# Attention, top-1 and Sinkhorn mixtures of experts in one kernel: the shared block's steps, the branch for further blocks and two weight loads in other places

## The chip, the cores and the metric

One NeuronCore of a Trainium2 chip runs the whole kernel. The metric is the device time of one execution in microseconds (us), the median of several runs; lower is better. TensorE is PE in the profile (its weight loads PEld), VectorE is DVE, ScalarE is ACT, GpSimd is POOL, SyncE is SP. SP and POOL also issue the transfers (DMAs): SP the plain ones, POOL the gathers and scatters by index.

## The reference

Attention with rotary positions over 2 batches, 8 heads, 576 positions of 64 values; its output, 1152 tokens of 512 values, goes through two layers of 8 experts. This change lies in and around the first of them:

```python
logits = xn @ en.T / tau                     # cosine of token and expert
expert_idx = np.argmax(logits, axis=1)
gate_w = probs[np.arange(N), expert_idx]
for e in range(E):
    mask = expert_idx == e
    h = np.maximum(x[mask] @ w1[e], 0.0)     # 512 -> 1024
    out[mask] = gate_w[mask, None] * (h @ w2[e])   # 1024 -> 512
```

The second layer (the dense one) puts every token through all 8 experts with weights from 8 Sinkhorn rounds.

## The kernel before, in words

**Stages.** Attention and routing come first (up to about 183 us of the span), then the expert blocks of the first layer (`run_blocks`, to about 340 us), then the dense layer (`dense_experts`, the rest). The instructions of PE, DVE, ACT and POOL stand in the order in which the Python code records them (`tc.manual_schedule`); each engine runs its own list in that order and waits where an operand isn't there.

**Blocks.** The tokens of an expert are cut into blocks of 128. Ten blocks (i = 0 to 9) always run; a branch (`tc.If`, L971) runs further ones if there are more than ten. Here there are not: after block 9 every engine jumps over that code. Experts with few tokens share one more block, 32 rows for each of four experts: the **shared block** (names with `quad`).

**One pass of the loop for block i** does on PE: L1(i), the first product (`block_l1`, L756, 24 matmuls); xt(i+1), four transposes of the next block's tokens (`block_x`, L743); L2(i-1), the second product of the block before (`block_l2`, L786); ht(i), eight transposes of L1's result (`block_turn`, L771). The products are made of fp32 values split in two: ACT copies the high parts (`whi` L728 of the weights, `xh` L746, `hh` L773) and DVE subtracts the low parts (`wlo` L721, `xl` L747, `hl` L774). Per pass there are two `whi`/`wlo` pairs for the next block's first weights and two for block i's second weights. DVE's two `hl` come behind the last two `wlo` of a pass.

**PSUM.** xt, ht and all small products of this stage take turns in two banks (tag "x"). A bank is free again when ACT and DVE have read it.

**The shared block.** `quad_fetch(s)` (s = 0 to 7) has SP load four 512 KB pieces of weights (`qw`) into a ring of eight tiles, so part s+2 can't be loaded before part s is multiplied. `place_quad` computes on DVE which token goes to which row (`slot`, L555), lets PE make the indices (ten small matmuls with `qv`, L561), and DVE writes them to `idx`. `block_in(NB)` has POOL gather the tokens, `quad_tokens` transposes them (`qxt`, L824), `quad_product(s)` is part s of the products (q0 to q7, L837, eight matmuls), `quad_relu` and `quad_turn` (L844, L851) come between parts 3 and 4. Before the change the places are computed in pass 1, and part s stands behind L2 in pass s+2; part 7 stands behind L1(9). Part s+1's load (`quad_fetch(i)` in pass i) is issued a whole pass and more ahead of its use.

**SP's queue** in a pass: the first weights of block i+2, the second weights of block i+1 (each 4 x 512 KB, left out when the expert stays the same; but SP still waits, at the first and third of them, until DVE's `wlo` has read the buffer), then the shared block's load. From pass 6 on `next(dense)` mixes in the dense layer's first steps: `fetch1(0)` and `fetch1(1)` load first weights (`raw1` from `w1b`, 512 KB a step), `prep_plain` splits them (L1032, L1033), and `fetch1(2)`, `fetch1(3)` load the next two as soon as their buffers are read.

**The change of stage.** Behind the branch SP loads four quarters of the layer's result (`g` from `yd`, L1151) once the last scatter into `yd` (POOL, L793) has landed; PE runs 28 matmuls to no purpose but activity (L1160) and then transposes the first quarter (L1163).

Of the kernel before, what the change touches and what calls it, by code (L numbers as in the profile page):

```python
# [10 lines left out]
F32 = mybir.dt.float32  # L11
# [38 lines left out]
def fused_kernel(ctx, tc, qk, vv, tab, cst, emb, tau, w1a, w2a, wg, w1b, w2b, out):  # L50
# [11 lines left out]
    def bank(tag, bufs, name, shape=(128, 512)):  # L62
        return ps[0].tile(list(shape), F32, tag=tag, bufs=bufs, name=name)
# [319 lines left out]
    def tmp(name, shape, dt=F32):  # L383
        return rt.tile(shape, dt, name=name)
# [5 lines left out]
    def over(v, axis, shape):  # L390
        return v.unsqueeze(axis).to_broadcast(shape)
# [151 lines left out]
            G.tensor_copy(qv[:, :, x], col(name))  # L543
        G.memset(qv[:, :, 5], 1.0)

    def place_quad(bank_):

        z, qi = tmp("z", [QT, E]), tmp("qi", [BLK, 2])
        V.tensor_scalar(z, grp, float(GS), 1024.0, op0=ALU.mult, op1=ALU.add)
        V.scalar_tensor_tensor(z, inq, -1024.0, z, op0=ALU.mult, op1=ALU.add)  # L550
        V.tensor_tensor(ws, ohb[:, :, :NQ], z.unsqueeze(1).unsqueeze(1).to_broadcast([QT, B, NQ, E]), op=ALU.mult)
        V.tensor_reduce(blk, ws, axis=AX.X, op=ALU.add)
        V.tensor_tensor(blk, blk, rk, op=ALU.add)
        sl = [QT, B * NQ, BLK]
        V.tensor_tensor(slot.rearrange("p b t n -> p (b t) n"), over(col("iota"), 1, sl),  # L555
                        over(blk.rearrange("p b t -> p (b t)"), 2, sl), op=ALU.is_equal)
        p = bank_()
        for b in range(B):
            for c in range(NQ):
                m, n = TW[c], b * NQ + c  # L560
                T.matmul(p[:, :6], slot[:m, b, c], qv[:m, n], start=(n == 0), stop=(n == B * NQ - 1))  # L561
        V.tensor_reduce(qi[:, 0:1], p[:, 0:2], axis=AX.X, op=ALU.add)
        V.tensor_copy(idx[:, 0, NB:], qi[:, 0:1])
        V.tensor_reduce(gate[:, NB:], p[:, 2:5], axis=AX.X, op=ALU.add)
        V.tensor_scalar(qi[:, 1:2], p[:, 5:6], 1.0, cs[:, COLS["slot"]], op0=ALU.subtract, op1=ALU.mult)
        V.tensor_tensor(qi[:, 1:2], qi[:, 0:1], qi[:, 1:2], op=ALU.subtract)
        V.tensor_copy(idx[:, 1, NB:], qi[:, 1:2])
# [253 lines left out]
    def quad_tokens():  # L821
        pt = bank("x", 2, "qxt")
        for k in range(KD_):
            T.transpose(pt[:, k * 128:(k + 1) * 128], quad["xb"][:, k * 128:(k + 1) * 128], ident)  # L824
        quad["x"] = mp.tile([128, F], F32, tag="qx", bufs=1, name="qx")
        A.activation(quad["x"][:, :DM], pt, AF.Copy)
# [19 lines left out]
    def quad_turn():  # L846
# [5 lines left out]
            A.activation(t[:, n * 512:(n + 1) * 512], pt, AF.Copy)  # L852
        quad["x"] = t

    def run_blocks(lo, hi, xb=None, w1=None, w2=None):

        def expert(i, raws, src, n):
# [9 lines left out]
        with tc.manual_schedule(engines=ORDERED):  # L867
# [10 lines left out]
            for i in range(lo, hi + 1):  # L878
                begin, here, more = i == 0, i < hi, i + 1 < hi

                if here:
                    p = block_l1(x, w1)
                if lo == 0 and i == 2:
                    quad_tokens()
                elif lo == 0 and i == 6:
                    quad_turn()
                elif lo == 0 and i == 9:
                    quad_product(7)
                    block_out(NB, quad["p", 0])
                if begin:  # L890
                    next(gated)
# [13 lines left out]
                if begin:  # L905
                    h = block_turn(hn)
                    split_low(raw2p[1], *w2[1])
                    w2 = pieces(w2)
                    expert(1, raw2, w2a, 256)
                    next(gated)  # L910
                    quad_fetch(0)
                    quad_constants()
                if i + 2 < hi and len(xb) < i + 3 - lo:
                    xb.append(block_in(i + 2))
                if begin:
# [7 lines left out]
                    y = block_l2(h, w2, (lambda: turned.append(block_turn(hn))) if i == hi - 1 else None, i == hi)  # L923
                if i == 1:
                    place_rest(lambda: bank("x", 2, "gp"))
                    place_quad(lambda: bank("x", 2, "gp"))
                    quad["xb"] = block_in(NB)
                if lo == 0 and 2 <= i <= 8:
                    quad_product(i - 2)
                    if i == 5:  # L930
                        quad_relu()
                if here:
                    s2 = split(raw2p)
                    next(s2)
# [2 lines left out]
                if here:  # L937
# [1 line left out]
                    w2 = next(s2)  # L939
                    expert(i + 1, raw2, w2a, 256)  # L940
                    h = turned[0] if i == hi - 1 else block_turn(hn)
                if lo == 0 and 1 <= i <= 7:
                    quad_fetch(i)
                if lo == 0 and i in (6, 7, 8, 9):
                    next(dense)
                    if i > 7:
                        next(dense)

    reg = [0]
    with tc.manual_schedule(engines=ORDERED | {mybir.EngineType.SP}):  # L950
# [18 lines left out]
        dense = dense_experts(ctx, tc, early, yd, wgk, w1b, w2b, out, ident, ones)  # L969
        run_blocks(0, NS, xb, pieces(first_w1), first_w2)  # L970
    with tc.If(nc.values_load(bei[0:1, NB:NB + 1], min_val=0, max_val=NB) > NS):  # L971
        run_blocks(NS, NB)
    mctx.close()


# [4 lines left out]
def dense_experts(ctx, tc, early, yd, wgk, w1b, w2b, out, ident, ones):  # L980
# [72 lines left out]
    def prep_plain(n):  # L1053

        for f in range(2):
            yield
            w1[n, f] = wtile(4)
            wsplit(w1[n, f], raw1[n][:, :, f])
        fetch1(n + 2)

    def prep1(n, part):

# [84 lines left out]
    for i in range(4):  # L1147
        if i % 2 == 0:
            gt = dp.tile([128, 4 * N], F32, tag="h", bufs=2, name="g")
        g = gt[:TQ, i % 2 * 3 * DM:(i % 2 + 1) * 3 * DM].rearrange("p (t d) -> p t d", t=3)  # L1150
        nc.sync.dma_start(out=g, in_=yd[i * QW:(i + 1) * QW].rearrange("(p t) d -> p t d", t=3))  # L1151
        gs.append(g)

    def turn_quarter(i, n):

# [351 lines left out]
```

## Time and profile before

| | us |
|---|---|
| median of 3 runs | 1127.99 (1127.86 to 1128.38) |
| the profiled execution, its own time | 1128.46 |
| its span, first to last instruction | 1126.7 |
| PE busy | 1097.5 |
| DVE busy | 777.4 |
| ACT busy | 467.8 |

The profile is of one execution, and durations are taken from it. A timeline row has its start, its busy time, engine, line, operation, output and inputs; in brackets stands how long the engine sat idle before it and who released it. Rows of equal instructions are merged (x4), and merged rows overlap a little, because matmuls are pipelined. The second of two neighbouring starts minus the first is therefore the better duration.

### The profile page before, as it was taken

The page shows a single profiled execution, that of the slowest core. Times are in us where ns is not written, and L with a number is a line of the kernel's source. Part 1 is how long each engine was busy: PE and PEld are TensorE (multiplying, and loading weights), DVE is VectorE, ACT ScalarE, POOL GpSimd, SP SyncE. Part 2 cuts the span into 40 slices and gives each one's busy share as a digit, 9 for nine tenths or more (in the row PEclk, how much of TensorE's full clock was granted, in tenths as well). Part 3 has the DMA queues.
Part 4 walks back from the last instruction along what each step waited for, and adds up shares of the span by engine and source line. Part 5 has one row for each costly group of instructions (what it writes and reads, how often), then busy time and mean ns, then how long its engine had stood idle before and what let it go on. Part 6 is the DMA issues. An engine that isn't in the chain of part 4 may idle for free.

```text
span 1126.7 us, 16883 instructions
## 1 busy us (share of the span) xinstructions
PE 1097.5 (97%) x6606; PEld 930.1 (83%) x6606; DVE 777.4 (69%) x1257; ACT 467.8 (42%) x742; POOL 131.6 (12%) x106
## 2 busy tenths in 40 slices
PE   8999996899998999999999999999999999999998
PEld 4777774776777988998889898898988898888987
DVE  5767768786763598766766667666676666776665
ACT  4656746486863442232322333323333233333330
POOL 7674403233210000000000000000000000000000
PEclk9999998899999999999999999999999999999999
DMA  8688613675735011111121111111111111111002
GB/s 243 181 229 258 180 33 123 223 264 207 228 117 152 20 57 56 38 38 38 56 57 38 38 38 57 53 41 39 38 56 44 51 38 38 57 39 56 19 1 84
DMA packets 74980, 102.09 MB, mean 91 GB/s; under 512 B 5128, under 2 KB 46600, under 8 KB 74128
## 3 DMA queue, kind: packets, MB, share of 16 engines
q1 hardware_dynamic: 72528, 94.12, 26.8%
q0 software_dynamic: 1760, 5.77, 1.6%
q8 instruction: 54, 0.88, 0.3%
q10 hardware_dynamic: 608, 1.07, 0.3%
q14 instruction: 30, 0.25, 0.1%
HBM read 110.31 MB, written 7.60 MB: 105 GB/s over the span
## 4 chain that ended last, share of the span: by engine, by line
PE 68%; DVE 1%; issue 0%
PE o L1320 35%; PE d L1266 29%; PE d L1283 2%; PE d L1160 1%; DVE acc L1326 0%; PE d L1163 0%; PE o L1210 0%; DVE h L1308 0%; DVE w L1033 0%; DVE w L1095 0%; PE o L1163 0%; DVE acc L1331 0%; DVE P L1245 0%; DVE rs L1234 0%; PE o L1241 0%
## 5 line engine op out<-in xcount | busy, mean ns | idle before, releaser
L1320 PE MATMUL o<-w,h 128*128 128x512 f32 x1728 | 435.6, 394 | 0.4 <-DVE acc L1326 0.4
L1266 PEld LDWEIGHTS d<-yq,w 128*128 128x128 f32 x2520 | 355.6, 188 | 17.9
L1266 PE MATMUL d<-yq,w 128*128 128x288 f32 x2520 | 367.3, 294 | 0.0
L1320 PEld LDWEIGHTS o<-w,h 128*128 128x128 f32 x1728 | 312.1, 188 | 57.8 <-DVE acc L1326 0.7
L1331 DVE SCALAR_TENSOR_TENSOR acc<-o,P,acc 128x512 f32<-128x512 f32 x252 | 189.1, 751 | 160.9 <-PE o L1320 160.9
L1307 ACT ACTIVATE h<-st 128x576 fp32r<-128x576 f32 x90 | 61.7, 685 | 217.2 <-DVE st L1297 217.2
L1294 ACT ACTIVATE st<-d 128x576 f32<-128x576 f32 x90 | 58.8, 653 | 219.5 <-PE d L1266 219.5
L721 DVE TENSOR_TENSOR wlo<-raw,whi 128x2048 fp32r<-128x2048 f32 x40 | 91.2, 2289 | 29.3 <-ACT whi L728 28.8
L1297 DVE TENSOR_TENSOR st<-st,d 128x576 f32<-128x576 f32 x90 | 67.6, 751 | 39.4 <-PE d L1266 39.4
L249 DVE TENSOR_REDUCE nb<-s 120x1 f32<-120x576 f32 (+1 forms) x80 | 60.3, 754 | 37.6 <-PE s L243 24.0
L1032 ACT ACTIVATE w<-raw 128x512 fp32r<-128x512 f32 x124 | 70.9, 574 | 19.4 <-DVE raw L1078 15.9
L255 ACT ACTIVATE p<-s,nb 120x576 f32<-120x576 f32 (+1 forms) x80 | 59.0, 738 | 46.8 <-DVE nb L249 44.6
L1033 DVE TENSOR_TENSOR w<-raw,w 128x512 fp32r<-128x512 f32 x124 | 76.7, 620 | 0.0
L728 ACT ACTIVATE whi<-raw 128x2048 fp32r<-128x2048 f32 x36 | 68.9, 1914 | 17.6 <-PE h L756 11.6
L1308 DVE SCALAR_TENSOR_TENSOR h<-st,h 128x576 fp32r<-128x576 f32 x90 | 67.5, 750 | 0.4 <-ACT h L1307 0.3
L243 PE MATMUL s<-kd,qd 128*120 128x288 f32 x280 | 54.5, 317 | 1.2 <-ACT p L255 1.2
L243 PEld LDWEIGHTS s<-kd,qd 128*120 128x120 f32 x280 | 38.6, 178 | 13.9 <-ACT ph L281 5.7
L300 PE MATMUL o<-ph,vr 120*64 120x288 f32 x320 | 46.8, 417 | 0.0
L283 DVE COPY ph<-pt 120x480 f32<-120x480 f32 x64 | 41.3, 647 | 2.2 <-PE pt L277 2.2
L1308 DVE SCALAR_TENSOR_TENSOR h<-d,h 128x576 fp32r<-128x576 f32 x38 | 28.8, 757 | 19.4 <-ACT h L1307 19.4
L1095 DVE TENSOR_TENSOR w<-raw,w 128x1024 fp32r<-128x1024 f32 x32 | 39.0, 1218 | 0.4 <-ACT w L1094 0.4
L277 PE MATMUL pt<-io,p 120*120 120x120 f32 x256 | 37.0, 267 | 1.2 <-DVE ph L283 1.2
(285 smaller groups left out, 1051.9 us busy)
## 6 DMA issues: line engine op xcount, KB each, us to landing
raw<-w1a SPq DMA_DIRECT2D x40, 512.0 KB
raw<-w2a SPq DMA_DIRECT2D x40, 512.0 KB
raw<-w1b SPq DMA_DIRECT2D x64, 256.0 KB
raw<-w2b SPq DMA_DIRECT2D x32, 512.0 KB
qw<-w1a SPq DMA_DIRECT2D x16, 512.0 KB
qw<-w2a SPq DMA_DIRECT2D x16, 512.0 KB
kd<-hl SPq DMA_DIRECT2D x28, 288.0 KB
r<-qk SPq DMA_DIRECT2D x6, 1152.0 KB
```

The costliest lines, as they stand in the source:

```text
L243: T.matmul(s[:m, h, :HS], qd[:, j, t * QT:t * QT + m], kd[:, j, x, h * HS:(h + 1) * HS], start=(x == 0), stop=(x == 1))
L249: V.tensor_reduce(nb[:m], s[:m, :, :HS], axis=AX.XY, op=ALU.max, negate=True)
L721: V.tensor_tensor(lo, raw, hi, op=ALU.subtract)
L728: A.activation(hi, raw, AF.Copy)
L1032: A.activation(hi, src, Copy)
L1033: V.tensor_tensor(lo, src, hi, op=ALU.subtract)
L1266: T.matmul(d[1][:, q, :QW], wv[:, wx, which, k], yq[yx][:, YQ[p], k, q * QW:(q + 1) * QW], start=new and k == 0 and (wx, yx) == (0, 0), st ...
L1297: V.tensor_tensor(halves(st[x]), halves(st[x]), mid(d), op=ALU.add)
L1307: A.activation(hi, src, AF.Relu)
L1308: V.scalar_tensor_tensor(lo, src, 0.0, hi, op0=ALU.max, op1=ALU.subtract)
L1320: T.matmul(d, hs[n][:, r, hx, t * 128:(t + 1) * 128], w2[n][:, wx, r], start=(r == 0 and (hx, wx) == (0, 0)), stop=(r == 1 and hx == 1))
L1331: V.scalar_tensor_tensor(a, d, p, a, op0=ALU.mult, op1=ALU.add)
```

## The change

Three things are moved. The shared block's places: DVE's part (`quad_slots`) stays in pass 1, PE's part, the indices and the gather (`place_quad`, `block_in(NB)`) go behind L1(2), and `quad_tokens` behind L2(1). The parts: q0 to q5 now stand behind L1(3) to L1(8), q6 behind L2(7) in pass 8, q7 behind L1(9) as before; `quad_relu` stands behind L1(6), `quad_turn` behind L2(5). The loads: part 1 in pass 1, parts 2 to 7 at the ends of passes 3 to 8. The code in the branch is new (`rest_of_blocks`, plain fp32 products from the loaded weights). One split of dense weights goes from pass 8 to pass 9, and `fetch1(2)`, `fetch1(3)` are written behind the loads of the quarters.

```diff
--- before.py
+++ after.py
@@ -543,9 +543,9 @@
             G.tensor_copy(qv[:, :, x], col(name))
         G.memset(qv[:, :, 5], 1.0)
 
-    def place_quad(bank_):
-
-        z, qi = tmp("z", [QT, E]), tmp("qi", [BLK, 2])
+    def quad_slots():
+
+        z = tmp("z", [QT, E])
         V.tensor_scalar(z, grp, float(GS), 1024.0, op0=ALU.mult, op1=ALU.add)
         V.scalar_tensor_tensor(z, inq, -1024.0, z, op0=ALU.mult, op1=ALU.add)
         V.tensor_tensor(ws, ohb[:, :, :NQ], z.unsqueeze(1).unsqueeze(1).to_broadcast([QT, B, NQ, E]), op=ALU.mult)
@@ -554,6 +554,10 @@
         sl = [QT, B * NQ, BLK]
         V.tensor_tensor(slot.rearrange("p b t n -> p (b t) n"), over(col("iota"), 1, sl),
                         over(blk.rearrange("p b t -> p (b t)"), 2, sl), op=ALU.is_equal)
+
+    def place_quad(bank_):
+
+        qi = tmp("qi", [BLK, 2])
         p = bank_()
         for b in range(B):
             for c in range(NQ):
@@ -852,6 +856,36 @@
             A.activation(t[:, n * 512:(n + 1) * 512], pt, AF.Copy)
         quad["x"] = t
 
+    def rest_of_blocks():
+
+        own = [nc.sync.value_load(bei[0:1, i:i + 1], min_val=0, max_val=E - 1) for i in range(NS, NB)]
+        for n, i in enumerate(range(NS, NB)):
+            for raws, src, m in ((raw1, w1a, 128), (raw2, w2a, 256)):
+                fetch(raws, src, m, own[n], None if n == 0 else own[n] != own[n - 1])
+            xb = block_in(i)
+            pt = bank("x", 2, "ext")
+            for k in range(KD_):
+                T.transpose(pt[:, k * 128:(k + 1) * 128], xb[:, k * 128:(k + 1) * 128], ident)
+            x = mp.tile([128, F], F32, tag="qx", bufs=1, name="ex")
+            A.activation(x[:, :DM], pt, AF.Copy)
+            p = bank("h", 1, "h", (128, 2, 512))
+            for k in range(KD_):
+                for c in range(2):
+                    T.matmul(p[:, c], x[:, k * 128:(k + 1) * 128], raw1[k][:, c * 512:(c + 1) * 512],
+                             start=(k == 0), stop=(k == KD_ - 1))
+            h = block_relu(p)
+            t = mp.tile([128, F], F32, tag="qx", bufs=1, name="eh")
+            for c in range(2):
+                pt = bank("x", 2, "eht")
+                for k in range(4):
+                    T.transpose(pt[:, k * 128:(k + 1) * 128], h[:, (4 * c + k) * 128:(4 * c + k + 1) * 128], ident)
+                A.activation(t[:, c * 512:(c + 1) * 512], pt, AF.Copy)
+            p = bank("y", 2, "y")
+            for k in range(KF):
+                T.matmul(p, t[:, k * 128:(k + 1) * 128], raw2[k // 2][:, k % 2 * 512:(k % 2 + 1) * 512],
+                         start=(k == 0), stop=(k == KF - 1))
+            block_out(i, p)
+
     def run_blocks(lo, hi, xb=None, w1=None, w2=None):
 
         def expert(i, raws, src, n):
@@ -880,12 +914,14 @@
 
                 if here:
                     p = block_l1(x, w1)
-                if lo == 0 and i == 2:
-                    quad_tokens()
-                elif lo == 0 and i == 6:
-                    quad_turn()
-                elif lo == 0 and i == 9:
-                    quad_product(7)
+                if i == 2:
+                    place_quad(lambda: bank("x", 2, "qp"))
+                    quad["xb"] = block_in(NB)
+                for q in {3: (0,), 4: (1,), 5: (2,), 6: (3,), 7: (4,), 8: (5,), 9: (7,)}.get(i, ()):
+                    quad_product(q)
+                if i == 6:
+                    quad_relu()
+                elif i == 9:
                     block_out(NB, quad["p", 0])
                 if begin:
                     next(gated)
@@ -909,7 +945,6 @@
                     expert(1, raw2, w2a, 256)
                     next(gated)
                     quad_fetch(0)
-                    quad_constants()
                 if i + 2 < hi and len(xb) < i + 3 - lo:
                     xb.append(block_in(i + 2))
                 if begin:
@@ -923,12 +958,14 @@
                     y = block_l2(h, w2, (lambda: turned.append(block_turn(hn))) if i == hi - 1 else None, i == hi)
                 if i == 1:
                     place_rest(lambda: bank("x", 2, "gp"))
-                    place_quad(lambda: bank("x", 2, "gp"))
-                    quad["xb"] = block_in(NB)
-                if lo == 0 and 2 <= i <= 8:
-                    quad_product(i - 2)
-                    if i == 5:
-                        quad_relu()
+                    quad_slots()
+                    quad_constants()
+                elif i == 2:
+                    quad_tokens()
+                elif i == 6:
+                    quad_turn()
+                elif i == 8:
+                    quad_product(6)
                 if here:
                     s2 = split(raw2p)
                     next(s2)
@@ -939,12 +976,10 @@
                     w2 = next(s2)
                     expert(i + 1, raw2, w2a, 256)
                     h = turned[0] if i == hi - 1 else block_turn(hn)
-                if lo == 0 and 1 <= i <= 7:
-                    quad_fetch(i)
-                if lo == 0 and i in (6, 7, 8, 9):
+                if i in (1, 3, 4, 5, 6, 7, 8):
+                    quad_fetch({1: 1, 3: 2, 4: 3, 5: 4, 6: 5, 7: 6, 8: 7}[i])
+                for _ in range({6: 1, 7: 1, 8: 1, 9: 3}.get(i, 0)):
                     next(dense)
-                    if i > 7:
-                        next(dense)
 
     reg = [0]
     with tc.manual_schedule(engines=ORDERED | {mybir.EngineType.SP}):
@@ -969,7 +1004,7 @@
         dense = dense_experts(ctx, tc, early, yd, wgk, w1b, w2b, out, ident, ones)
         run_blocks(0, NS, xb, pieces(first_w1), first_w2)
     with tc.If(nc.values_load(bei[0:1, NB:NB + 1], min_val=0, max_val=NB) > NS):
-        run_blocks(NS, NB)
+        rest_of_blocks()
     mctx.close()
 
 
@@ -1056,7 +1091,6 @@
             yield
             w1[n, f] = wtile(4)
             wsplit(w1[n, f], raw1[n][:, :, f])
-        fetch1(n + 2)
 
     def prep1(n, part):
 
@@ -1150,6 +1184,8 @@
         g = gt[:TQ, i % 2 * 3 * DM:(i % 2 + 1) * 3 * DM].rearrange("p (t d) -> p t d", t=3)
         nc.sync.dma_start(out=g, in_=yd[i * QW:(i + 1) * QW].rearrange("(p t) d -> p t d", t=3))
         gs.append(g)
+    for n in (2, 3):
+        fetch1(n)
 
     def turn_quarter(i, n):
 
```

DVE in pass 1, from the slots on (`qi` and `idx` are the shared block's indices, `gp` and `qp` the bank that PE's ten small matmuls write). Before:

```order
L555 TENSOR_TENSOR slot<-cs,blk 120x1280
L562 TENSOR_REDUCE qi<-gp 128x1
L563 CAST idx<-qi 128x1
...
L567 CAST idx<-qi 128x1
L721 TENSOR_TENSOR wlo<-raw_79,whi 128x2048
L721 TENSOR_TENSOR wlo<-raw_80,whi 128x2048
L774 TENSOR_TENSOR hl__2478<-ht,hh 128x512 x2
```

Now:

```order
L555 TENSOR_TENSOR slot<-cs,blk 120x1280
L725 TENSOR_TENSOR wlo<-raw_79,whi 128x2048
L725 TENSOR_TENSOR wlo<-raw_80,whi 128x2048
L778 TENSOR_TENSOR hl__2458<-ht,hh 128x512 x2
L566 TENSOR_REDUCE qi<-qp 128x1
L567 CAST idx<-qi 128x1
...
L571 CAST idx<-qi 128x1
```

The index writes moved behind the two weight splits and both `hl`.

ACT in passes 5 and 6 (`h<-q` is `quad_relu`, `qh` is `quad_turn`, `h<-h` the relu of a block). Before:

```order
L844 ACTIVATE h<-q 128x512 x2
L728 ACTIVATE whi<-raw_79 128x2048
L792 ACTIVATE y<-y,gate 128x512
L728 ACTIVATE whi<-raw_80 128x2048
L773 ACTIVATE hh<-ht 128x512 x2
L852 ACTIVATE qh<-qht 128x512 x2
L728 ACTIVATE whi<-raw_77 128x2048
L762 ACTIVATE h<-h 128x1024
```

Now:

```order
L777 ACTIVATE hh<-ht 128x512 x2
L848 ACTIVATE h<-q 128x512 x2
L732 ACTIVATE whi<-raw_77 128x2048
L766 ACTIVATE h<-h 128x1024
L732 ACTIVATE whi<-raw_78 128x2048
L750 ACTIVATE xh<-xt 128x512
L856 ACTIVATE qh<-qht 128x512 x2
L732 ACTIVATE whi<-raw_79 128x2048
```

`h<-q` moved to the head of pass 6, ahead of its first `whi`, and `qh` behind `xh`.

SP's last rows ahead of the branch (`raw_79` and `raw_80` are the second weights of block 9, `qw` the shared block's last load, `w1b` the steps 2 and 3 of the dense weights). Before:

```order
L817 DMA qw<-w2a 128x2x512
L84 REGISTER_ALU x2
...
L84 DMA raw_80<-w2a 128x2x512
L1044 DMA raw_3433<-w1b 128x4x128 x2
L1044 DMA raw_3532<-w1b 128x4x128 x2
L971 COMPARE_AND_BRANCH
...
L1151 DMA g<-yd 96x1536 x4
```

Now:

```order
L84 DMA raw_80<-w2a 128x2x512
L821 ISA
L821 DMA qw<-w2a 128x2x512
...
L1079 DMA raw_3968<-w1b 128x4x128 x2
L1079 DMA raw_3971<-w1b 128x4x128 x2
L1006 COMPARE_AND_BRANCH
...
L1185 DMA g<-yd 96x1536 x4
```

The shared block's last load moved from ahead of block 9's second weights to behind them; the two steps of `w1b` stand ahead of the branch and of `g` in both.

## Rows read from the trace of the kernel before

**Rows 1.** The page: busy time, share of the span and instructions by engine.
```profile
PE 1097.5 (97%) x6606; PEld 930.1 (83%) x6606; DVE 777.4 (69%) x1257; ACT 467.8 (42%) x742; POOL 131.6 (12%) x106
```

**Rows 2.** Waits of PE (waiting, releaser: us in total, times, longest).
```profile
PE gp L561 <- DVE slot L555: 3.3, 1, 3.3
```

**Rows 3.** Timeline of PE, passes 1 to 3 (start, busy us, engine, line, ...).
```profile
213.19 0.42 PE L561 MATMUL gp<-qv,slot 120*128 120x6 bf16 x10 [3.30 <-DVE slot L555]
213.47 1.96 PE L771 MATMUL ht<-io,h 128*128 128x128 f32 x8
...
222.19 0.48 PE L786 MATMUL y<-whi,hh 128*128 128x512 f32 x1
...
227.82 1.92 PE L837 MATMUL q<-qw,qx 128*32 128x512 f32 x16
229.68 1.12 PE L771 MATMUL ht<-io,h 128*128 128x128 f32 x8
230.55 0.70 PE L756 MATMUL h<-whi,xh 128*128 128x512 f32 x2
...
236.48 0.48 PE L786 MATMUL y<-whi,hh 128*128 128x512 f32 x1
```

**Rows 4.** Busy time by stretch: PE, PEld, DVE, ACT, POOL, granted clock, DMA share, GB/s.
```profile
210.00:220.00 10.00, 6.81 (x36) 5.79 (x37) 9.14 (x19) 3.56 (x4) 4.86 (x2) 0.83 0.34 131
```

**Rows 5.** Timeline of DVE, pass 1.
```profile
211.64 1.49 DVE L555 TENSOR_TENSOR slot<-cs,blk 120x1280 bf16<-120x1280 f32 x1
...
214.53 4.50 DVE L721 TENSOR_TENSOR wlo<-raw,whi 128x2048 fp32r<-128x2048 f32 x2
218.94 1.28 DVE L774 TENSOR_TENSOR hl__2478<-ht,hh 128x512 fp32r<-128x512 f32 x2
```

**Rows 6.** Timeline of POOL: the shared block's gather.
```profile
214.73 2.90 POOL L736 DMA_INDIRECT xb<-xd,idx  x1 [25.48 <-DVE idx L567]
```

**Rows 7.** Stretches of 0.25 us: the last in which that gather moved data.
```profile
219.50:219.75 0.25, 0.25 (x3) 0.21 (x2) 0.25 (x2) 0.00 (x0) 0.25 (x1) 1.00 0.13 49
```

**Rows 8.** Timeline of PE, ACT and DVE, passes 5 to 7.
```profile
272.80 0.60 ACT L844 ACTIVATE h<-q 128x512 f32<-128x512 f32 x1 [0.26 <-PE q L837]
280.56 1.25 PE L851 MATMUL qht<-io,h 128*128 128x128 f32 x8 [1.40 <-DVE hl__3014 L774]
282.35 1.91 ACT L728 ACTIVATE whi<-raw 128x2048 fp32r<-128x2048 f32 x1
289.21 0.69 DVE L747 TENSOR_TENSOR xl<-xt,xh 128x512 fp32r<-128x512 f32 x1
290.66 0.71 PE L756 MATMUL h<-whi,xh 128*128 128x512 f32 x2
```

**Rows 9.** Timeline of SP: the last load of qw, and block 9's second weights.
```profile
308.09 2.26 SPq L817 DMA_DIRECT2D qw<-w2a  x4
318.72 3.29 SPq L84 DMA_DIRECT2D raw<-w2a  x4
```

**Rows 10.** Stretches of 0.5 us: the last in which that load of qw moved data.
```profile
316.00:316.50 0.50, 0.50 (x3) 0.19 (x1) 0.50 (x2) 0.00 (x0) 0.00 (x0) 1.00 0.20 78
```

**Rows 11.** Timeline of PE, passes 8 and 9: q6 behind L2(7), and q7.
```profile
316.56 1.92 PE L837 MATMUL q<-qw,qh 128*32 128x512 f32 x16
...
324.92 1.92 PE L837 MATMUL q<-qw,qh 128*32 128x512 f32 x16
```

**Rows 12.** Timeline of all engines at the branch.
```profile
339.58 1.80 SPq L1044 DMA_DIRECT2D raw<-w1b  x2
340.65 0.97 POOL L793 DMA_INDIRECT yd<-y,idx  x1 [4.28 <-ACT y L792]
342.86 8.23 PE L1160 MATMUL d<-w 128*128 128x512 f32 x28 [3.26 <-PEq L971]
346.33 0.21 POOL L1139 MEMSET lw<- 128x128 f32 x1 [4.71 <-DMA yd<-y,idx]
350.94 1.03 PEld L1163 LDWEIGHTS d<-io,g 96*128 96x128 f32 x12 [0.27 <-DMA g<-yd]
```

## The prediction

> **What bounds the kernel now.** I read the page first, then the waits of PE, then the timelines around the places that the diff touches. The page's busy line shows PE at 97%, far ahead of DVE at 69% [rows 1]: of a span of 1126.7 us PE was idle for 1126.7 − 1097.5 = 29.2. A step moved on another engine is worth nothing unless it shortens such a pause or a slow stretch of PE, or makes a new one. Behind 343 us the diff changes nothing in PE's work, so I look at the expert blocks, at four places.
>
> PE's longest wait of this kind is 3.3 us for `slot` [rows 2]. Its timeline shows that the ten small matmuls of the shared block's places start at 213.19 after 3.30 of idleness, so PE had been free at 209.89 [rows 3]. What follows is slow as well: from the start of ht(1) at 213.47 to that of L2(1) at 222.19 pass 8.72 us; one pass later the same ht takes 229.68 to 230.55 = 0.87, and L1 with xt 230.55 to 236.48 = 5.93 [rows 3]. With some 0.44 for `qxt`, which is half as many transposes as ht, that makes 7.24; so 1.5 us are lost to a clock that was 0.83 in that stretch [rows 4].
>
> **The change part by part.**
>
> *Places and gather, passes 1 and 2.* The wait for `slot` goes: from 209.89 ht(1) 0.87 and L1(2) 5.5 (5.93 less xt) run at once, to 216.3. What is late next is the bank for the small matmuls: it was last ht(1)'s, and `hl`, which reads it, stands on DVE behind `slot` (to 213.13) and two `wlo`, whose start lies 4.41 before that of `hl` [rows 5]. So `hl` starts at 217.5, its first half ends 0.64 later at 218.2, the second at 218.8, and PE idles 1.9 where it idled 3.3. The small matmuls take 0.28 [rows 3]; xt(3) waits for the second `hl`; L2(1) starts at 219.3 and ends 5.63 later (222.19 to 227.82 before, [rows 3]) at 224.9.
>
> The gather loses its cover. Before, `idx` lay there long before POOL got to it: POOL had idled 25.48 until that write [rows 6]; the gather began at 214.73 and moved its last data by 219.75, 5.0 us [rows 7]. It began 1.54 after the small matmuls, 1.26 without their 0.28. Now DVE can write the indices only behind the second `hl`, so it starts at 218.8 + 1.26 = 220.1 and lands at 225.1, just behind L2(1). Then come `qxt` 0.44, ACT's copy of it (0.60 for such a shape [rows 8], some 0.3 to start) and what filled 227.82 to 236.48 before, 8.66: L2(2) at 235.1 instead of 236.48. I take **−1.4**. Bounds: without the bank's wait 232.6, −3.9; if the clock falls after this pause as it did after 3.30, the 1.5 come back, +0.1.
>
> *Relu and transposes of the shared block, passes 5 and 6.* Before, L1(6) ended at 279.16, then PE waited 1.40 for `hl` ahead of `qht`, and L1(7) began at 290.66, 11.5 later [rows 8]. Now `qht` needn't wait for that, but `h<-q` stands ahead of pass 6's first `whi` on ACT: q3 takes 1.86 (227.82 to 229.68 for such a part, [rows 3]), the copy of its second half starts 0.26 later and takes 0.60 [rows 8], so it ends 2.7 after L1(6). From the first `whi` to the end of `xl` the chain lasted 282.35 to 289.90 = 7.55 [rows 8]; it now ends at 10.2, and ht(6)'s second half takes the bank that `xl` reads, so L1(7) starts some 0.8 later, as it did behind `xl` before, at 11.0. Thus **−0.5**; bounds −1.9 (the wait of 1.40 gone and no new one) and +1.0 (the clock falls in the new wait, 1.5).
>
> *q7 and its load, passes 8 and 9: the term that decides.* Part 7's load was issued at 308.09, ahead of block 9's second weights, whose rows run on SP from 318.72 for 3.29, to 322.01, because their buffers come free only as DVE's `wlo` reads them [rows 9]. Now it is issued behind them, at 322.01 at the earliest. Its last data moved by 316.5, 8.4 after its first issue [rows 10]. So it lands at 330.4. L2(7) ended at 316.56 and q7 began at 324.92 [rows 11]; that time stays, as q6 now stands behind L2(7) again and L1(9) behind that. q7 is late by 330.4 − 324.92 = 5.5; since PE can do the matmuls of the pieces that are there, about 0.6 of them is done by then: **+4.9** (bounds +4.0, if the pieces land well before the last one, and +6.0). A pause of that length comes with the slow clock seen after 3.30 [rows 4], 1.5 there: **+1.5** (bounds 0 and 2.0). The 2 MB lie in plain rows; by the Trainium skill (DMA: Bandwidth & Descriptors, section on the anatomy of a SWDGE DMA) an estimate for 2.1 MB would be 2.0 + 4.8 = 6.8 us instead of the row's 8.4, and the kernel would be some 1.6 us faster than I say; that fit is for transfers which GpSimd issues, and I stay with the row.
>
> *The end of the stage.* The order of SP shows that steps 2 and 3 of `w1b` are still issued ahead of the branch and of `g`, though they are written behind: here the change doesn't do what it says. What moves is that both now go out with the last of pass 9, 1 MB beside the scatter into `yd`. Before, one pair was issued at 339.58, the scatter at 340.65, and POOL saw it landed at 346.33; the first quarter reached PE at 350.94, with 0.27 of waiting left behind the 28 idle matmuls of 8.23 [rows 12]. There is nothing to spare there: half a megabyte more is a quarter of the load that took 8.4, so up to 2 us if it came before `g` entirely. I take **+0.4**, since most of it runs while the scatter has its own latency; bounds 0 and +1.5.
>
> *The branch's code* is shorter. PE waited 3.26 for its sequencer at the jump [rows 12]. Even if that vanished, the chain to `g` (scatter, landing, load) sets the end here, and 0.27 is all that it can give; I count 0. The Trainium skill (Runtime: NRT & Kernel Launch, Instruction fetch mechanics) says that a jump whose target isn't in the loaded code pages has to fetch it first; the row's 3.26 agrees with that, and by the rule the wait stays wherever the target lies beyond the fetched pages.
>
> *Nothing for the rest.* q0 to q5 stand one pass later with loads that still go out a pass or more ahead; the split moved to pass 9 lies on ACT and DVE, which have slack (42% and 69%, [rows 1]); bounds for this last ±0.5.
>
> **Sum:** −1.4 − 0.5 + 4.9 + 1.5 + 0.4 = +4.9. The execution profiled took 1128.46, 0.47 above the median of 1127.99; so 1133.4 for such an execution, 1132.9 as a median.
>
> **The rivals.**
> A, *the last load is in time.* It decides at 8.4 us between SP's issue and q7: by the rows it is 324.92 − 322.01 = 2.9. For it speaks only that SP's waits in pass 8 may end sooner when other steps have moved. Then −1.4 − 0.5 + 0.4 = −1.5: 1126.5, within 0.2% (chance 0.06). If the two waits for banks were absent also, −3.9 − 1.4 + 0.4 = −4.9: 1123.1, faster (0.10). Against the latter speaks the order of DVE, `hl` behind two `wlo`.
> B, *q7 is late, but the waits for banks are absent:* −4.9 + 4.9 = 0 without a loss of clock, 1128.0, +1.5 with it, 1129.5; within 0.2% (0.14).
> C, *the clock falls in each new pause, and w1b delays the quarters:* +0.1 + 1.0 + 4.9 + 1.5 + 1.5 = +9.0: 1137.0, slower (0.14). For it speaks that 3.30 of idleness cost 1.5 before; against it, that the new pauses are 1.9 and about 1.
>
> **How the numbers follow.** My own case has 0.56: 1132.9, with its own range of 1130.5 to 1135.5. What a measurement can tell from no change is about 0.2%, 2.3 us. A's second half gives 0.10 faster; A's first half and B give 0.20 the same; my case and C give 0.70 slower. The range leaves out A's 0.16 and the far end of C: 1128.0 to 1138.0.
>
> **What would show it.** In the changed profile: a wait of PE at the small matmuls for `hl` of about 1.9, none for `slot`; the wait of 1.40 ahead of `qht` gone and a wait for `xl` or ACT in its place, about 1; above all PE waiting some 5 us at q7 for the DMA into `qw`, which SP issues behind block 9's second weights, and a granted clock below 1 behind it; the first quarter reaching PE slightly later. I am wrong if `qw`'s last load goes out 8 us or more ahead of q7, if its pieces are there within 3 us, or if PE passes the small matmuls without a pause.

## The result, and the profile after

The changed kernel takes 1136.26 us (1135.11 to 1138.41, 4 runs), the kernel before 1127.98: a ratio of 1.0075, 95% interval 1.0058 to 1.0092. It is slower by 8.3 us, where the text above expected 4.9. The profiled execution took 1138.41, its span is 1136.6; it is the longest of the four, so the parts read from it below add up to more than 8.3.

The page's busy line of the changed kernel:

```profile
PE 1103.6 (97%) x6606; PEld 932.6 (82%) x6606; DVE 777.2 (68%) x1257; ACT 468.4 (41%) x742; POOL 129.8 (11%) x106
```

Its waits of PE (waiting, releaser: us in total, times, longest):

```profile
PE d L1196 <- PEq L1006: 4.3, 1, 4.3
...
PE q L841 <- DMA qw<-w2a: 2.9, 4, 1.6
PE qxt L828 <- DMA xb<-xd,idx: 1.8, 1, 1.8
PE qp L565 <- DVE hl__2458 L778: 1.6, 1, 1.6
```

The engines do the same work as in [rows 1], but PE is busy 6.1 us longer: matmuls took longer, on top of the waits. The 3.3 of [rows 2] is gone; in its place stand 1.6 for `hl`, 1.8 for the gather and 2.9 for `qw`.

To see where the time came from, I cut each profile at five starts: the last small matmuls of `place_rest` (gp from ib, L476), xt(4), q6, the last scatter into `yd`, and PE's transposes of the first quarter. Each number is the difference of two starts in a timeline.

| us | place_rest to xt(4) | place_rest to q6 | q6 to scatter | scatter to quarter | quarter to end |
|---|---|---|---|---|---|
| before | 26.63 | 107.07 | 24.09 | 10.29 | 775.76 |
| after | 30.10 | 110.02 | 30.14 | 11.99 | 775.84 |
| difference | +3.47 | +2.95 | +6.05 | +1.70 | +0.08 |

Up to place_rest's matmuls the changed kernel was 0.88 earlier (208.61 instead of 209.49). That start lies between 207.24 and 209.99 in all the profiles of this study, whatever the kernel, so nothing is read into it. The sum is −0.88 + 2.95 + 6.05 + 1.70 + 0.08 = +9.9, as the two spans have it (1136.6 − 1126.7).

**Passes 1 to 3.** PE's timeline, which answers to [rows 3]:

```profile
208.61 0.40 PE L476 MATMUL gp<-ib,slot 120*128 120x16 bf16 x10
209.11 1.06 PE L775 MATMUL ht<-io,h 128*128 128x128 f32 x8
...
217.31 0.41 PE L565 MATMUL qp<-qv,slot 120*128 120x6 bf16 x10 [1.65 <-DVE hl__2458 L778]
217.90 0.66 PE L747 MATMUL xt<-io,xb 128*128 128x128 f32 x4 [0.19 <-DVE qi L566]
218.31 0.62 PE L790 MATMUL y<-whi,hh 128*128 128x512 f32 x1
...
227.39 0.63 PE L828 MATMUL qxt<-io,xb 128*128 128x128 f32 x4 [1.78 <-DMA xb<-xd,idx]
228.71 1.97 PE L775 MATMUL ht<-io,h 128*128 128x128 f32 x8 [0.69 <-ACT qx L830]
...
236.85 1.92 PE L841 MATMUL q<-qw,qx 128*32 128x512 f32 x16
```

Up to L2(1) it goes as forecast: ht and L1(2) at once, then 1.65 for `hl`, L2(1) 9.7 behind place_rest's matmuls (forecast 219.3 − 209.5 = 9.8). Then the clock falls and the gather is late. The clock, by stretch (PE, PEld, DVE, ACT, POOL busy, granted clock, DMA share, GB/s):

```profile
219.00:221.00 2.00, 2.00 (x6) 1.52 (x6) 2.00 (x2) 0.19 (x1) 2.00 (x1) 0.50 1.02 412
...
229.00:231.00 2.00, 2.00 (x10) 1.90 (x9) 0.51 (x1) 2.00 (x3) 0.00 (x0) 0.50 0.02 4
```

0.50 is the lower of its two levels, once behind the pause for `hl`, and again behind those for the gather and `qx`. In the first stretch the transfer engines are full, 412 GB/s, while the gather is on its way: POOL issued it at 218.85 and its data came for PE at 227.39, 8.5 later, where [rows 6, 7] had 5.0.

**q7** in PE's timeline, as against [rows 11]:

```profile
327.89 1.05 PE L841 MATMUL q<-qw,qh 128*32 128x512 f32 x2 [0.82 <-DMA qw<-w2a]
329.19 1.05 PE L841 MATMUL q<-qw,qh 128*32 128x512 f32 x2 [0.26 <-DMA qw<-w2a]
331.80 1.05 PE L841 MATMUL q<-qw,qh 128*32 128x512 f32 x2 [1.56 <-DMA qw<-w2a]
333.10 1.90 PE L841 MATMUL q<-qw,qh 128*32 128x512 f32 x10 [0.25 <-DMA qw<-w2a]
```

SP issued the load at 324.35. PE begins with each piece as it lands. But a lone pair takes 1.05, and the ten that are left for the last piece take 1.90, as long as all sixteen do when everything is there (1.92, [rows 11]). What PE did ahead of the last piece saved nothing: q7 ends 1.9 behind that landing whatever came before. The single starts within the last row fit the reason: four at 333.10, four at 333.55, one at 333.98, one at 334.41. Each piece holds the weights of one of the four experts, and each expert has four of the sixteen matmuls in the rows. Those of different experts start together, those of one expert one after another, and the expert whose piece comes last has all four still to do. The waits show 2.9 of the loss, the rest is hidden in busy time.

**The change of stage**, as against [rows 12], in the timeline of SP, PE and POOL:

```profile
347.10 2.12 SPq L1079 DMA_DIRECT2D raw<-w1b  x4
355.78 1.95 SPq L1185 DMA_DIRECT2D g<-yd  x4
...
352.05 8.01 PE L1196 MATMUL d<-w 128*128 128x512 f32 x28 [4.33 <-PEq L1006]
360.76 1.21 PE L1199 MATMUL d<-io,g 96*128 96x96 f32 x12 [0.70 <-DMA g<-yd]
...
348.77 0.97 POOL L797 DMA_INDIRECT yd<-y,idx  x1 [4.27 <-ACT y L796]
355.94 0.21 POOL L1173 MEMSET lw<- 128x128 f32 x1 [6.20 <-DMA yd<-y,idx]
```

The scatter landed 7.17 behind its start instead of 5.68, `g` was issued 7.01 behind it instead of 5.75.

### The profile page after: what moved, and what is told of

Same layout as the page of the kernel before. It is cut to its first block, busy times and chain, and to the rows that moved or that the text cites. A ratio compares the mean times of both kernels' runs of the same rounds, so it can differ in the third digit from the quotient of the medians.

```text
span 1136.6 us, 16884 instructions
## 1 busy us (share of the span) xinstructions
PE 1103.6 (97%) x6606; PEld 932.6 (82%) x6606; DVE 777.2 (68%) x1257; ACT 468.4 (41%) x742; POOL 129.8 (11%) x106
## 3 DMA queue, kind: packets, MB, share of 16 engines
q0 software_dynamic: 1760, 5.77, 1.5%
## 4 chain that ended last, share of the span: by engine, by line
PE 66%; DVE 1%; DMA 0%; issue 0%; another core or an unknown queue 0%; SPq 0%
PE o L1356 35%; PE d L1302 29%; PE d L1319 2%; DMA g<-yd 0%; DVE acc L1362 0%; PE d L1199 0%; PE o L1246 0%; PE d L1196 0%; DVE h L1344 0%; DVE w L1068 0%; DVE w L1129 0%; PE o L1199 0%; DVE acc L1367 0%; DVE P L1281 0%; DVE rs L1270 0%
```

## The experiments

All start from the changed kernel, but b1. Executions of one kernel differ by up to 5.8 us (e5), so the table of starts above often tells more than a median; every run below is read by both.

**e1: the last load early.**

```diff
                     quad_product(q)
+                if i == 8:
+                    quad_fetch(7)
...
-                if i in (1, 3, 4, 5, 6, 7, 8):
-                    quad_fetch({1: 1, 3: 2, 4: 3, 5: 4, 6: 5, 7: 6, 8: 7}[i])
+                if i in (1, 3, 4, 5, 6, 7):
+                    quad_fetch({1: 1, 3: 2, 4: 3, 5: 4, 6: 5, 7: 6}[i])
```

> The changed kernel, with the shared block's last load issued right behind q5 in pass 8, ahead of block 9's second weights on SP. Theory (the late load costs 6.1 us, from q7 wanted at 327.0 to the landing of its last piece at 333.1): PE's waits for qw vanish, q7 runs in 1.9 at once, and the time falls by 6.1, from 1136.3 to 1130.2 (1129 to 1131.5). Rival (the load is late, but what it delays would wait anyway at the change of stage, for the scatter and the quarters): at most 2 us less, 1134.3 or more.

Measured: 1130.6 (1129.68 to 1134.44), 5.7 less; against the kernel before beside it the ratio is 1.0025 instead of 1.0075. q6 to scatter is 24.08, as before. So the late load is 5.7 of the 8.3 us (6.05 of the 9.9 in the profile), and nothing behind it would have absorbed them. PE's timeline of e1:

```profile
325.34 1.93 PE L841 MATMUL q<-qw,qh 128*32 128x512 f32 x16
...
343.82 9.42 PE L1198 MATMUL d<-w 128*128 128x512 f32 x28 [3.80 <-PEq L1008]
```

**e2: w1b's loads where they were**, in `prep_plain` and behind `g`.

```diff
             wsplit(w1[n, f], raw1[n][:, :, f])
+        fetch1(n + 2)
...
-    for n in (2, 3):
-        fetch1(n)
```

> The changed kernel, with fetch1(2) and fetch1(3) back in prep_plain. Theory (1 MB of w1b beside the last scatter makes it land 7.2 instead of 5.7 us after its start, so the first quarter reaches PE 1.7 later): scatter to landing 5.7 again, and 1.7 less, 1134.6. Rival (the load of w1b is not what delays the scatter; SP's own lateness or the code behind the branch is): landing stays at 7 us, 1136.3 within 0.8.

Measured: 1135.79 (1135.48 to 1137.38). The scatter landed within 5.04, yet scatter to quarter was 11.68, hardly less than 11.99. The landing is the theory's, the time the rival's, so neither holds whole. Two pairs of w1b were issued beside the scatter here too (344.70 to 348.28, the scatter at 346.38), so the edit moved nothing, and the load doesn't as such delay the landing. Nor is the landing what `g` waits for. SP issued `g` 1.7 behind it, as the timeline of SP and POOL in e2 shows:

```profile
344.70 3.58 SPq L1079 DMA_DIRECT2D raw<-w1b  x4
353.15 1.89 SPq L1186 DMA_DIRECT2D g<-yd  x4
...
351.42 0.21 POOL L1174 MEMSET lw<- 128x128 f32 x1 [4.08 <-DMA yd<-y,idx]
```

From the end of SP's last w1b issue to `g` there are 353.15 − 348.28 = 4.87. Before, it was 346.40 − 341.38 = 5.02 [rows 12], in e1 4.77. Between the two SP only passes the branch. So the new theory: SP's last issue ahead of the branch sets `g`, some 4.9 later, and that issue is late because one split moved from pass 8 to pass 9 and SP then has two pairs to issue there instead of one. In the one profile of the changed kernel the landing, 7.17, came later still than this; in the other profiles with that split moved (e1 to e4, e11, b1) it took 5.0 to 5.8, `g` went out 6.5 to 7.2 behind the scatter all the same, and scatter to quarter is 11.1 to 12.0. In e1 the idle matmuls, 9.42 long, end as late as that (343.82 + 9.42 = 353.24, the quarter starts at 353.08 without a wait), so there they set the quarter, and `g` is late beside them.

**e3: the old places with the new order of parts.**

```diff
                 if i == 2:
-                    place_quad(lambda: bank("x", 2, "qp"))
-                    quad["xb"] = block_in(NB)
+                    quad_tokens()
...
                     quad_slots()
-                    quad_constants()
-                elif i == 2:
-                    quad_tokens()
+                    place_quad(lambda: bank("x", 2, "gp"))
+                    quad["xb"] = block_in(NB)
```

(`quad_constants()` is back behind `quad_fetch(0)`.)

> The changed kernel, with the small matmuls, the indices and the gather back in pass 1 behind place_rest, and the tokens' transposes behind L1(2). Theory (the new places cost 3.5 us between the end of place_rest's matmuls and L2(2): the wait for hl, a gather of 7 us without cover, and two stretches at a granted clock of 0.5): 3.3 of waiting for slot comes back, those go, L2(2) 27.4 behind the small matmuls of place_rest as before instead of 30.1; 2.6 to 3.5 less, 1133.2. Rival (the new places gain 1.4 as forecast and the loss between the two is some disturbance of one profile): 1137.7.

Measured: 1138.39 (1137.35 to 1139.1), 2 more instead of 3 less. place_rest to xt(4) is 28.41, 1.8 above before, though the places are the same. What is new there, and q7, in PE's timeline of e3:

```profile
229.57 0.66 PE L775 MATMUL ht<-io,h 128*128 128x128 f32 x4 [1.78 <-DVE xl L751]
...
331.36 4.56 PE L841 MATMUL q<-qw,qh 128*32 128x512 f32 x12 [2.21 <-DMA qw<-w2a]
```

Before, q0 stood between L2(1) and ht(2) and covered that wait: 1.86 of work against 1.78. With q0 behind L1(3) it is bare. So places and parts can't be judged apart; moving the parts alone costs 1.8. And q7's last twelve matmuls took 4.56, where the same twelve take 3.20 in the changed kernel (331.80 to 335.00, a wait included): the granted clock behind the pause was 0.50. That is 1.4 of the 2.1 by which q6 to scatter is longer, 32.26 instead of 30.14; the third piece also came 0.8 later.

**e4: the old code in the branch.**

```diff
-        rest_of_blocks()
+        run_blocks(NS, NB)
```

> The changed kernel, with the old code in the branch (never entered here). Theory (the code that is jumped over plays no part, the sequencer's 4.33 instead of 3.26 comes from transfers beside it): 1136.3 within 0.8. Rival (its length sets the wait at the jump): the wait of PE's sequencer 3.3 again, but g is late anyway, so at most 0.5 less.

Measured: 1137.05 (1135.11 to 1138.97), the changed kernel's time. PE's sequencer waited 4.00. It is 3.26, 3.48 and 4.00 in the three profiles with the old code, 3.20 to 4.33 in the others, so no part of the length of the code that is jumped over is to be seen. q7 fell to the low clock here too (12 matmuls in 4.42), and q6 to scatter was 31.56.

**e5: e1 and e2's edit, with the split back in pass 8:**

```diff
-                for _ in range({6: 1, 7: 1, 8: 1, 9: 3}.get(i, 0)):
+                for _ in range({6: 1, 7: 1, 8: 2, 9: 2}.get(i, 0)):
```

**e7: e1 with w1b truly behind g** (the lines in between indented):

```diff
     gs = []
-    for i in range(4):
+    with tc.manual_schedule(engines=ORDERED | {mybir.EngineType.SP}):
+        for i in range(4):
...
-    for n in (2, 3):
-        fetch1(n)
+        for n in (2, 3):
+            fetch1(n)
```

> e1 with the split of dense weights back in pass 8 and both fetch1 back in prep_plain, so SP has one pair of w1b transfers less to issue ahead of the branch. Theory (g is issued some 4.9 after SP's last transfer of w1b, which the moved split makes later by 1 to 1.5): g issued 5.7 to 5.8 after the scatter instead of 6.8, the first quarter at PE 10.3 after it instead of 12.0; 1.7 less than e1, 1128.9. Rival (the shorter code behind the jump or the idle matmuls at half clock make the delay): unchanged, 1130.6.

> e1 with fetch1(2) and fetch1(3) truly behind the loads of g (the order of SP fixed there), as the change was written. Theory as for e5: SP reaches the branch before the scatter starts, g is issued as soon as the scatter has landed, 5.1 to 5.7 after its start, and the first quarter is at PE 10 to 10.3 after it; 1128.6 to 1129. Rival (the second and third products then wait for w1b, or the landing is the limit anyway): 1130.6 or more.

**b1: the kernel before with only that split moved:**

```diff
-                if lo == 0 and i in (6, 7, 8, 9):
-                    next(dense)
-                    if i > 7:
-                        next(dense)
+                if lo == 0:
+                    for _ in range({6: 1, 7: 1, 8: 1, 9: 3}.get(i, 0)):
+                        next(dense)
```

> The kernel before with one thing changed: one split of dense weights in pass 9 instead of pass 8. Theory: SP's last transfer of w1b goes out 1 to 1.5 later, g with it, and the time rises by 1 to 1.7, to 1129.2 to 1129.9. Rival (the split has nothing to do with it): 1128.2 within 0.5.

Measured: scatter to quarter 10.58 in e5, 10.07 in e7, 11.64 in b1, against 12.02 in e1 and 10.29 before. `g` was issued 5.77, 4.09 and 6.85 behind the scatter; from SP's last w1b issue to `g` 4.59 in e5 and 4.92 in b1. In e7, where no such issue stands ahead, `g` goes with the landing (345.41 and 345.50), and by 343.53 + 8.02 the idle matmuls set the quarter; in e5 they do too (345.30 + 8.22 = 353.52, the quarter at 353.36). For the issue of `g` the profiles bear the theory out on both sides. What the late `g` costs in time they leave open, for the medians don't resolve it: 1130.29 and 1130.63, the rivals' figure, where 1128.9 and 1128.6 to 1129 were expected, and for b1 1129.14 beside 1128.8 (ratio 1.0009, 1.0000 to 1.0018), 0.3 more where 1 to 1.7 was expected, in runs that spread over 3 to 6 us. Against the kernel before beside each, e1 is 1.0025, e5 1.0012 and e7 1.0020, with intervals that overlap. SP's timeline of b1:

```profile
337.62 3.61 SPq L1043 DMA_DIRECT2D raw<-w1b  x4
346.15 1.89 SPq L1150 DMA_DIRECT2D g<-yd  x4
```

**e11: the load of part 1 a pass later.**

```diff
-                if i in (1, 3, 4, 5, 6, 7, 8):
-                    quad_fetch({1: 1, 3: 2, 4: 3, 5: 4, 6: 5, 7: 6, 8: 7}[i])
+                if i in (2, 3, 4, 5, 6, 7, 8):
+                    quad_fetch({2: 1, 3: 2, 4: 3, 5: 4, 6: 5, 7: 6, 8: 7}[i])
```

> The changed kernel, with the load of part 1 issued at the end of pass 2 instead of pass 1, so that it isn't in flight beside the shared block's gather. Theory (the forecast's 5.0 us for that gather came from a time when the transfer engines were idle; now 2 MB of qw are issued 1.5 us before it): from the gather's start to the first of the tokens' transposes less than 6.8 us, which is where L2(1) ends, instead of 8.5; PE's wait for the gather gone; from place_rest's matmuls (gp from ib) to L2(2) 28.7 or less instead of 30.5; 1.8 to 3.5 less in all, 1134.0. Rival (the gather itself, with its places on POOL's queue, takes 8 us here): unchanged 30.5 and 1136.3.

Measured: 1134.76 (1134.46 to 1135.05), 1.5 less by the medians, 2.3 by the ratios to the kernel before (1.0055 instead of 1.0075); place_rest to xt(4) 26.36 instead of 30.10. The transfers are 0 GB/s from 218 to 222, and the gather's last data move by 224.0, 5.1 behind its issue, as before the change. The timeline of POOL and PE in e11:

```profile
218.90 2.92 POOL L740 DMA_INDIRECT xb<-xd,idx  x1 [7.34 <-issue]
...
217.35 0.40 PE L565 MATMUL qp<-qv,slot 120*128 120x6 bf16 x10 [1.87 <-DVE hl__2458 L778]
...
225.37 0.60 PE L828 MATMUL qxt<-io,xb 128*128 128x128 f32 x4
226.65 1.09 PE L775 MATMUL ht<-io,h 128*128 128x128 f32 x8 [0.69 <-ACT qx L830]
```

The same gather, issued at the same time, no wait behind L2(1), and ht(2) at the full clock (1.09 instead of 1.97). The six profiles with the new places and that load ahead of the gather (the changed kernel, e1, e2, e4, e5, e7) have 27.81 to 30.10 for this stretch, the two without it (e11, e12) 26.36 and 26.49. So the changed kernel's loss in these passes against the kernel before comes from that one load.

**e12: all three loads mended** (e1, e7 and e11 together).

> The changed kernel with its places and parts as they are, but all three loads mended: part 7's behind q5 (e1), steps 2 and 3 of w1b behind g (e7), part 1's at the end of pass 2 (e11). Theory (the loads are the whole loss): from place_rest's matmuls to q6 106.3 as in e11, q6 to the last scatter 24.1 as in e1, scatter to first quarter 10.1 as in e7; against the kernel before 0.8 + 0 + 0.2 = 1.0 less, 1127.7. Rival (something else of the change costs time, hidden so far behind the late loads): 1130 or more.

Measured: 1128.44 beside 1128.12 before, ratio 0.9994 (0.9984 to 1.0004). place_rest to q6 is 106.42 and scatter to quarter 10.55, but q6 to scatter is 26.10, not 24.1: q6 now waits for its own load. PE's timeline of e12:

```profile
315.40 1.77 PE L841 MATMUL q<-qw,qh 128*32 128x512 f32 x6
317.46 1.90 PE L841 MATMUL q<-qw,qh 128*32 128x512 f32 x10 [0.28 <-DMA qw<-w2a]
```

So the three loads were the loss: with them mended the kernel is level with the one before. What places and parts alone would bring isn't shown, since part 6's load, late in its turn, holds back 2.0 us here (q6 takes 315.40 to 319.36, 3.96 instead of 1.92).

**e6, e9, e10: other places.** e6 is e5 with the places a pass later; there part 2's load goes out at the end of pass 4, part 3's behind q1. e9 has e7's order of w1b instead, and part 2's load right behind q0. e10 adds the last four lines.

```diff
+                if i == 4:
+                    quad_tokens()
-                if i == 2:
+                if i == 3:
                     place_quad(lambda: bank("x", 2, "qp"))
...
-                for q in {3: (0,), 4: (1,), 5: (2,), 6: (3,), 7: (4,), 8: (5,), 9: (7,)}.get(i, ()):
+                for q in {5: (1,), 6: (3,), 7: (4,), 8: (5,), 9: (7,)}.get(i, ()):
...
                 elif i == 2:
-                    quad_tokens()
+                    quad_slots()
+                elif i == 4:
+                    quad_product(0)
+                elif i == 5:
+                    quad_product(2)
...
-                    y = block_l2(h, w2, (lambda: ...) if i == hi - 1 else None, i == hi)
+                    y = block_l2(h, w2, (lambda: ...) if i == hi - 1 else (lambda: quad_turn((0,))) if i == 6 else None, i == hi)
...
-                    quad_turn()
+                    quad_turn((1,))
```

> e5 with the shared block's places a pass later: slots on DVE behind xl of pass 2, small matmuls and gather behind L1(3), tokens' transposes behind L1(4), q0 behind L2(3), q1 behind L1(5), q2 behind L2(4), then as in e5, with the loads to match. Theory (in passes 1 and 2 the changed kernel loses by waits for hl and for the gather, and the clock that falls with them): PE runs from place_rest's matmuls to L2(2) without a pause, some 23 to 24 instead of 28 to 30 (without q0 there, 1.9); 1124 to 1125.5, faster than before. Rival (DVE itself is the limit in pass 1 and 2, so the wait moves to xt(3) or ht(2); or the loads of parts 2 and 3 come late): 1127 or more.

> e6 with the load of part 2 right behind q0 in pass 4, ahead of block 5's second weights, and with fetch1(2), fetch1(3) behind g as in e7. Theory: q2, which waits for its load in e6 and takes 5.6 instead of 1.9, runs at once; from place_rest's matmuls to q6 103.6 instead of 107.3 (before: 107.1), scatter to first quarter 10.1; 1124 to 1125, faster than before by 3.5. Rival (block 5's second weights, behind it now, come late for their split): a new wait for whi or wlo in pass 5, 1127 or more.

> e9 with the first four of the shared block's transposes in the middle of L2(5), the others behind it. Theory: PE's two waits of 0.69 for the copy qh shrink to one of about 0.4; 1.0 less than e9. Rival (the bank that the first half takes comes free too late in the middle of L2(5)): as e9 or slower by up to 1.

Measured: e6 1127.46 (ratio 0.9994, 0.9985 to 1.0003), e9 1125.53 (0.9964, 0.9949 to 0.9978), e10 1123.9 (0.9955, 0.9942 to 0.9968). place_rest to q6 is 107.27, 103.63 and 102.61. In e6 the passes 1 to 3 have one pause of 1.15 for `hl` left of the old ones, but part 2's load came late, as the rival had it: q2 took from 266.07 to 271.66, 5.6 instead of 1.9. PE's timeline of e6, then of e9:

```profile
266.07 2.22 PE L841 MATMUL q<-qw,qx 128*32 128x512 f32 x4
268.55 1.04 PE L841 MATMUL q<-qw,qx 128*32 128x512 f32 x2 [0.25 <-DMA qw<-w1a]
269.83 1.91 PE L841 MATMUL q<-qw,qx 128*32 128x512 f32 x10 [0.23 <-DMA qw<-w1a]
```

```profile
229.60 0.41 PE L565 MATMUL qp<-qv,slot 120*128 120x6 bf16 x10 [1.11 <-DVE hl__2581 L778]
...
265.20 1.92 PE L841 MATMUL q<-qw,qx 128*32 128x512 f32 x16
```

From place_rest to q6 e10 is 1.02 shorter than e9, as expected, but only one of the two waits for `qh` is gone (0.69; the other is still 0.69 long). The other 0.3 is q3, which took 2.24 in e9 and 1.92 here. e10 is the fastest kernel here, 4.8 below the 1128.7 of the kernel before beside it. Against the forecast for e9 some is missing at q6, which waits about 1 for part 6's load now that all stands earlier.

## Why the prediction was right or wrong

**q7, right in place, price by chance.** Forecast 4.9, and 1.5 for the clock, 6.4; measured 6.05 in the profile, 5.7 between the medians. The issue came 5.7 behind q6 (forecast 5.5), the landing 8.75 behind that (8.4). The Trainium skill's fit (DMA: Bandwidth & Descriptors, anatomy of one SWDGE DMA), an estimate of 6.8, was the worse guide. The step "about 0.6 of them is done by then" failed: nothing is saved ahead of the last piece. The clock's 1.5 wasn't in the profile shown (1.00 throughout), but e3 and e4 have it: twelve matmuls of q7 in 4.56 and 4.42 instead of 3.20, 1.4 and 1.2 more. It comes in some executions. So 6.4 is near 6.05 because 1.5 too much for the clock and some 1.2 too little for the rest (6.05 − 4.9) nearly cancel.

**Places and gather, wrong in sign.** Forecast −1.4, at most +0.1; measured +3.47. Two terms were missized. That the gather "moved its last data by 219.75, 5.0 us" was taken as its duration; the row was right, but in that stretch nothing else moved, and in the changed order the load of part 1 goes out 1.5 ahead of it; 8.5 came instead. e11 shows that this is the cause of the loss: without that load the passes cost 26.36, 0.3 less than before. And the clock, which I held as a bound for one pause, fell behind both. The second fall (ht(2) 1.97 long instead of 1.09) is in e1, e2 and e7 too, a little later in e5, and not in e4, where place_rest to xt(4) took 27.81.

**Relu and transposes, right in size, not in what sets it.** xt(4) to q6 went from 80.44 to 79.92, −0.5 as forecast. But PE's waits are as long as they were, twice 0.69 for `qh` instead of 1.40 for `hl`, and the wait for `xl` at the end of ACT's chain, from which the −0.5 was worked out, isn't there. The bound of −1.9 for that wait gone and nothing in its place should have been −1.4, as rivals A and B have it. From the end of L1(6) to L1(7) it is 11.2 instead of 11.5; the other 0.2 lies in the other passes. PE's timeline of the changed kernel:

```profile
288.65 0.66 PE L855 MATMUL qht<-io,h 128*128 128x128 f32 x4 [0.69 <-ACT qh L856]
290.00 1.09 PE L775 MATMUL ht<-io,h 128*128 128x128 f32 x8 [0.69 <-ACT qh L856]
290.84 0.71 PE L760 MATMUL h<-whi,xh 128*128 128x512 f32 x2
```

That q0 to q5 cost nothing one pass later held too, but only beside the new places: with the old ones e3 has the bare wait of 1.78.

**The change of stage, too small, and the mechanism only in part.** Forecast +0.4 for the scatter's landing beside w1b, at most 1.5; measured +1.70. In the profile shown the landing was late indeed, and `g` went out with it (355.78, the landing seen at 355.94). But e1 to e4 have the same load beside the scatter and the landing in 5.0 to 5.8, and still no early quarter. The limit on `g` there is SP, whose last w1b issue ends 4.6 to 5.3 ahead of `g`, and the moved split, which I had costed at nothing for ACT and DVE, delays it through the loads that SP issues behind it. That PE's wait at the jump is no matter of code length is what e4 shows. The Trainium skill (Runtime: NRT & Kernel Launch, Instruction fetch mechanics) has a taken jump fetch its target where that lies outside the code that is loaded, with which waits of 3.2 to 4.3 agree for either code. That the same is what holds SP is inferred from its timeline, not shown.

**In sum**, the direction came from the term that decides; the size (8.3 instead of 4.9) was short by the gather and the change of stage. 1136.26 lies outside the own case's 1130.5 to 1135.5 and nearest to rival C, 1137.0, which had the clock fall in each new pause and w1b delay the quarters. That C comes so near is luck as well: the gather cost 3.4 more than its +0.1, and its +1.0 for the relu and 1.5 for q7's clock aren't in the profile.

## What to carry to other kernels

A transfer moved behind a waiting instruction on its queue can't start before that wait ends, so its lateness is read from the queue's rows. Work that is shared out like q7's ends a full run behind the last piece, however much came earlier. A transfer's duration from the trace holds only beside what flew with it: look at what the new order issues just ahead. Where stages meet at a branch, ask which engine arrives there last, the one that only issues included.

## What the runs showed of the hardware

The granted clock fell to 0.50 behind pauses of PE of 1.65 (the changed kernel), 1.87 (e1, e11) and 3.30 (before), but stayed at 1.00 behind one of 1.86 in e2 and one of 1.78 in e3. In q7 it stayed at 1.00 in the changed kernel, where PE idled 2.9 in four pieces between short runs of matmuls; in e3 and e4, with last pauses of 2.21 and 1.34 there, it fell to 0.50. The 28 idle matmuls behind the branch took 8.0 to 8.3 in most profiles, with the clock at 0.50 for a part of them (before: 344 to 346). In e1 and e10, where it stayed there longer (e1: 344 to 348 and beyond), they took 9.4 and 9.5.

This goes with the distance between executions of one kernel. Of 31 executions of the kernel before, run beside e5, the 14 with a mean granted clock of 0.989 or 0.990 took 1128.55 to 1129.81, the 14 with 0.992 took 1126.91 to 1128.80. Of the 11 of e12, the four with 0.993 or 0.994 took 1125.27 to 1126.48, the other seven, with 0.989 to 0.991, 1128.28 to 1129.58.
